# Two matmul layers behind a decayed attention: a planner that ranks by simulated passes and also places TensorE's steps

## The chip, the core and the metric

The kernel runs on one core of a Trainium2 chip. The metric is the device time of one launch, in microseconds; the median of three runs before the change is 581.78 us (581.52 to 581.89). "Profile" is one execution recorded by the hardware profiler. The engines are PE (TensorE), DVE (VectorE), ACT (ScalarE), POOL (GpSimd) and SP (SyncE, which here only starts transfers). Each takes its instructions strictly in the order in which the program put them.

## The reference, cut to what matters

Attention first, in blocks of 64 positions with a decayed running state, over 2 batches, 8 heads, 768 positions and a head size of 64:

```python
for b in range(nb):                       # 12 blocks of 64
    intra = (qb @ kb.T * Dmask) @ vb
    inter = (qb * lam_pow) @ kv_state
    out[block b] = intra + inter
    kv_state = lam_block * kv_state + (kb * rev_pow).T @ vb
x = out as 1536 tokens x 512
h = x @ w_in;  g = where(h > 0, h, exp(min(h, 0)) - 1);             x = g @ w_out    # layer 0
h = x @ w_in;  g = max(h, 0) + alpha * min(h, 0);                   x = g @ w_out    # layer 1
```

`w_in` is 512x2048 and `w_out` 2048x512 in both layers. Everything is float32; the kernel gets the products' precision from three passes over operands split into a high and a low part (hi*hi, hi*lo, lo*hi), names ending in `h` and `l`.

## The kernel before

**Attention** runs in six units `m` of 128 positions of both batches. Each unit has four steps on PE: `scores` (L557, 32 matmuls of 64x64), `state` (L604), `outputs` (L644) and `earlier` (L668, the part that comes from the running state, in two pieces of 16). Around them DVE multiplies scores by the mask (`sm`, L565) and adds to the state (L630), ACT or POOL decays the state (L623, L626), POOL scales keys and queries (`kd` L575, `qs` L586), ACT and DVE split the result into high and low parts (`qbh` L374, `qbl` L696, `x0h`, `x0l`). The trace shows two records for each 64x64 matmul, and a weight load record for each.

**The layers.** Tokens are in three tiles `t` of 512. Up products of tile 0 (and of all tiles for the first weight step `j`=0) are plain: groups of six 128x512 matmuls (L815, operands `x0` or `qb`, weights `wa`). Tiles 1 and 2 otherwise share seven products of a Strassen-like scheme (L845): A11, A12, S1, S2, S4, S3, A22 in that order, where the S products use `ws` (weight sums) and `qT1` to `qT3` (token differences). DVE joins their banks in L859; ACT and DVE apply the activation (L762, L773, L775, L779) and split it (`g`, high part by ACT L374, low part by POOL or DVE L382). Down products (L895) read `g` and `wd`, and DVE adds their banks to `acc` (L906). Weights arrive as 64-bit words (`raw`, L362) and are converted by ACT L408 and DVE L410, L413, L416 into `wt`, then split into `wa`, `wd`, `ws` (L374, L382). At the start of each layer `combine` subtracts quarters of `acc` (acc<-acc, L382) and splits the results into `qT1` to `qT3`.

**Order.** The program first only lists steps (`Plan.add`), each with a cost for every engine that could take it. `needs` walks back from the end and gives each step the latest time at which it may start; PE's own steps are a fixed chain in the order in which the program listed them, which `merge` laid out by hand (up products and down products in turn). `run` then plays the steps forward once: each engine but PE takes the ready step that is needed first, PE takes its next one in the list. DVE and POOL exclude one another on steps marked `shared`. Two rules steer POOL and DVE: POOL holds back from a step if DVE has a more urgent shared one due within `HOLD` (8 us), and DVE leaves a step to POOL while it has more than `SPARE` (8 us) of slack. What `run` emits is the program.

Of the kernel before, what the change touches and what calls it, by code (L numbers as in the profile page):

```python
# [43 lines left out]
class Op:  # L44
    def __init__(self, costs, run, late, shared, dma):
        self.costs, self.run, self.late, self.shared, self.dma = costs, run, late, shared, dma
        self.least = min(costs.values())
        self.after, self.before = set(), []
        self.heir, self.waits = None, 0
        self.left = 0  # L50
        self.need = 0.0
        self.begun = False


class Plan:

    LAT = 0.12
    SPARE = 8.0  # L60
    EASE = 0.3
    HOLD = 8.0
# [6 lines left out]
    def add(self, costs, run, reads=(), writes=(), late=0.0, shared=False, dma=False):  # L69
        op = Op(costs, run, late, shared, dma)  # L70
# [12 lines left out]
    def behind(self, a, b):  # L83

        a.heir, b.waits = b, 1

    def needs(self):

        pe = [op for op in self.ops if "PE" in op.costs]
        behind = dict(zip(pe, pe[1:]))  # L90
        left = {}
        for op in self.ops:
            for a in op.after:
                a.before.append(op)
        for op in self.ops:
            left[op] = len(op.before) + (op in behind) + (op.heir is not None)
        todo = [op for op in self.ops if not left[op]]
        ahead = dict(zip(pe[1:], pe))
        first = {op.heir: op for op in self.ops if op.heir}
        n = 0  # L100
        while todo:
            op = todo.pop()
            n += 1
            ends = [s.need - (0.0 if "PE" in op.costs and "PE" in s.costs else self.LAT)
                    for s in op.before]
            if op in behind:
                ends.append(behind[op].need)
            op.need = min(ends, default=0.0) - op.least - op.late
            if op.heir:
                op.need = min(op.need, op.heir.need - op.least)  # L110
            for a in [*op.after, *([ahead[op]] if op in ahead else []),
                      *([first[op]] if op.waits else [])]:
                left[a] -= 1
                if not left[a]:
                    todo.append(a)
        assert n == len(self.ops)
        return pe

    def run(self):
        pe = self.needs()  # L120
        for op in self.ops:
            op.left = len(op.after) + op.waits
# [3 lines left out]
        events, n = [], 0  # L126
        at, done, now, dma, shift = 0, 0, 0.0, 0.0, -pe[0].need
# [13 lines left out]
        def begin(e, op):  # L141
            nonlocal dma
            op.begun = True
            op.run(e)
            if op.heir:
                op.heir.left -= 1
                if not op.heir.left:
                    offer(op.heir)
            cost = op.costs[e]
            free[e] = now + cost  # L150
# [3 lines left out]
            if op.dma:  # L154
                dma = max(dma, now + 1.6) + op.late
                wake(dma + self.LAT, op)
            else:
                wake(now + cost + (0.0 if e == "PE" else self.LAT), op)

        for op in self.ops:  # L160
            if not op.left:
                offer(op)
        while done < len(self.ops):
            for e in self.ENGINES:
                if free[e] > now + 1e-9:
                    continue
                if e == "PE":
                    if at < len(pe) and not pe[at].left:
                        shift = now - pe[at].need
# [4 lines left out]
                while ready[e]:  # L174
                    item = heapq.heappop(ready[e])
                    op = item[2]
                    if op.begun:
# [4 lines left out]
                    if e == "POOL" and any(  # L182
                            x.shared and not x.begun and x is not op and x.need < op.need
                            and x.need + shift < now + op.costs[e] + self.HOLD for _, _, x in ready["DVE"]):
# [3 lines left out]
                    slack = op.need + shift - now  # L188
# [10 lines left out]
            while events and events[0][0] <= now + 1e-9:  # L199
# [4 lines left out]
                for s in op.before:  # L204
                    s.left -= 1
                    if not s.left:
                        offer(s)

# [18 lines left out]
def attention_two_layers(  # L227
# [124 lines left out]
    def pe(cost, run, reads, writes):  # L352
        return plan.add({"PE": cost}, lambda e: run(), reads, writes)
# [144 lines left out]
    ATT = 0.95  # L498
# [51 lines left out]
    def scores(m):  # L550

        ks = two_banks(m, 0)
        for b, x in enumerate(units[m]):
# [7 lines left out]
            pe(ATT / 2, run, [x.b_kq], [b_ps[k] for k in ks])  # L561
# [31 lines left out]
    def state(m):  # L593
# [14 lines left out]
        pe(ATT, run, [*b_kd[m % 2], *[x.b_v for x in units[m]]], [b_ps[k] for k in ks])  # L608
# [27 lines left out]
    def outputs(m):  # L636
# [13 lines left out]
        pe(ATT, run, [*b_sm[m % 2], *[x.b_v for x in units[m]]], [b_ps[k] for k in ks])  # L650
# [8 lines left out]
    def earlier(m, ks):  # L659

        for s in range(2):
            k = ks[s]
            if m or s:
# [10 lines left out]
                last[m] = pe(ATT / 2, run, [b_st[(2 * m + s) % 4], *b_qs[m % 2]], [b_ps[k]])  # L674
# [436 lines left out]
```

## Time and profile before

| | |
|---|---|
| median of three runs | 581.78 us |
| the profiled execution, as timed | 581.23 us |
| its span in the trace | 579.3 us |
| PE busy | 550.4 us, 95% of the span |
| DVE, ACT, POOL busy | 383.0, 293.1, 339.2 us |
| the chain of work that ended last | PE 85%, DVE 9% of the span |

The profiled execution was timed 1.9 us above its span and 0.55 us below the median. PE is the engine with the least idle time, so the page is to be read by asking where PE stands still, and behind whom. The 40 slices show it idle in the first four (attention), and full from the fifth to the last but for single tenths.

### The profile page before, as it was taken

How to read it: one execution, taken by the hardware profiler on the slowest of the kernel's cores; microseconds unless marked ns; L12 is line 12 of the kernel's file. 1: busy time of each engine (PE TensorE's matmuls, PEld its weight loads, DVE VectorE, ACT ScalarE, POOL GpSimd, SP SyncE). 2: the span in 40 equal slices, each digit the busy share in tenths (PEclk: the TensorE clock that was granted, in tenths of full speed). 3: DMA queues.
4: the chain of work that ended last, by engine and by line, in shares of the span. 5: the costliest groups of instructions: out<-in, count | busy, mean ns of one | idle time of the engine just before them, and what ended most of it. 6: DMA issues, size and time to landing. Idle time of an engine off the chain costs nothing.

```text
span 579.3 us, 9092 instructions
## 1 busy us (share of the span) xinstructions
PE 550.4 (95%) x3712; PEld 457.1 (79%) x3712; DVE 383.0 (66%) x494; ACT 293.1 (51%) x474; POOL 339.2 (59%) x231
## 2 busy tenths in 40 slices
PE   7557999899999999999999999999999999999997
PEld 6457787788888888888878878788888888888886
DVE  3346679955866675757884688467776776765464
ACT  2326668585746464646562554664453443534320
POOL 4457152658767566564475886767859293946020
PEclk9778999999999999999999999999999999999999
DMA  8992032103122212221240100222332222000013
GB/s 320 393 291 77 20 129 74 46 30 143 41 106 74 72 74 72 74 72 74 72 147 1 35 39 1 73 74 73 98 120 74 72 74 72 1 0 1 36 38 145
DMA packets 20012, 49.62 MB, mean 86 GB/s; under 512 B 1282, under 2 KB 1538, under 8 KB 19970
## 3 DMA queue, kind: packets, MB, share of 16 engines
q1 hardware_dynamic: 19696, 48.51, 24.3%
q8 instruction: 29, 0.48, 0.3%
q10 hardware_dynamic: 274, 0.52, 0.3%
q14 instruction: 13, 0.11, 0.1%
HBM read 45.88 MB, written 3.15 MB: 85 GB/s over the span
## 4 chain that ended last, share of the span: by engine, by line
PE 85%; DVE 9%; issue 4%; DMA 1%; ACT 1%; SPq 0%; ACTq 0%
PE ps L895 41%; PE ps L845 20%; PE ps L815 18%; PE ps L668 2%; PE ps L604 1%; PE ps L557 1%; PE ps L644 1%; DMA blk<-in_vk 1%; DVE g L382 1%; DVE wt L413 1%; DVE qbl L382 1%; DVE wt L416 1%; DVE wdl L382 1%; DVE ps L859 1%; DVE acc L906 1%
## 5 line engine op out<-in xcount | busy, mean ns | idle before, releaser
L906 DVE TENSOR_TENSOR acc<-ps,acc 128x512 f32<-128x512 f32 (+1 forms) x169 | 116.1, 687 | 93.5 <-PE ps L895 92.6
L382 POOL TENSOR_TENSOR g<-rt,g 128x512 fp32r<-128x512 f32 x81 | 121.2, 1503 | 90.1 <-ACT g L374 88.0
L895 PE MATMUL ps<-wdh,g 128*128 128x512 f32 (+1 forms) x388 | 118.7, 387 | 1.4 <-DVE g L382 1.4
L895 PE MATMUL ps<-g,wdh 128*128 128x512 f32 x384 | 118.3, 389 | 0.0
L762 ACT ACTIVATE rt<-ps 128x512 f32<-128x512 f32 x96 | 57.3, 599 | 107.8 <-DVE ps L859 62.6
L895 PEld LDWEIGHTS ps<-wdh,g 128*128 128x128 f32 x388 | 72.7, 188 | 16.7 <-DVE g L382 1.9
L895 PEld LDWEIGHTS ps<-g,wdh 128*128 128x128 f32 x384 | 72.1, 188 | 15.0
L895 PE MATMUL ps<-wdl,g 128*128 128x512 f32 (+1 forms) x194 | 75.1, 387 | 0.0
L895 PE MATMUL ps<-g,wdl 128*128 128x512 f32 x192 | 74.8, 390 | 0.2 <-DVE wdl L382 0.2
L374 ACT CAST g<-rt 128x512 fp32r<-128x512 f32 x96 | 59.3, 618 | 28.7 <-DVE rt L775 14.4
L382 POOL TENSOR_TENSOR wsl<-wt,wsh 128x1024 fp32r<-128x1024 f32 x13 | 32.3, 2484 | 48.1 <-ACT wsh L374 30.5
L779 DVE SCALAR_TENSOR_TENSOR rt<-rt,beta,ps 128x512 f32<-128x512 f32 x48 | 35.7, 744 | 30.2 <-ACT rt L762 30.1
L382 POOL TENSOR_TENSOR wt<-wt 128x256 f32<-128x256 f32 x54 | 41.1, 778 | 10.4 <-DVE wt L416 4.8
L416 DVE SCALAR_TENSOR_TENSOR wt<-raw,wt 128x1024 uint32<-128x1024 uint32 x32 | 46.3, 1450 | 0.0
L413 DVE SCALAR_TENSOR_TENSOR wt<-raw,wt 128x1024 uint32<-128x1024 uint32 x32 | 45.6, 1429 | 0.2
L374 ACT COPY ut<-ps 128x512 f32<-128x512 f32 x42 | 24.6, 587 | 36.3 <-PE ps L845 36.1
L382 POOL TENSOR_TENSOR wdl<-wt,wdh 128x1024 fp32r<-128x1024 f32 x13 | 37.2, 2861 | 8.9 <-ACT wdh L374 8.7
L895 PEld LDWEIGHTS ps<-g,wdl 128*128 128x128 f32 x192 | 36.0, 188 | 7.9 <-DVE wdl L382 0.6
L895 PEld LDWEIGHTS ps<-wdl,g 128*128 128x128 f32 x194 | 36.4, 188 | 7.4
L859 DVE TENSOR_TENSOR ps<-ps,ut 128x512 f32<-128x512 f32 x42 | 29.2, 697 | 14.5 <-PE ps L845 14.3
L815 PE MATMUL ps<-x0l,wah 128*128 128x512 f32 x128 | 38.8, 389 | 0.0
L775 DVE SCALAR_TENSOR_TENSOR rt<-rt,ps 128x512 f32<-128x512 f32 x48 | 32.5, 681 | 8.7 <-ACT rt L773 8.0
(116 smaller groups left out, 948.6 us busy)
## 6 DMA issues: line engine op xcount, KB each, us to landing
raw<-in_w1i SPq DMA_DIRECT2D x8, 1024.0 KB, 5.5
raw<-in_w1o SPq DMA_DIRECT2D x8, 1024.0 KB, 4.9
raw<-in_w2i SPq DMA_DIRECT2D x8, 1024.0 KB, 5.5
raw<-in_w2o SPq DMA_DIRECT2D x8, 1024.0 KB, 4.9
blk<-in_kqT SPq DMA_DIRECT2D x11, 512.0 KB, 10.8
blk<-in_vk SPq DMA_DIRECT2D x10, 512.0 KB, 10.9
out<-acc SPq DMA_DIRECT2D x11, 256.0 KB, 2.0
blk<-in_kqT ACTq DMA_DIRECT2D x1, 512.0 KB, 5.3
```

Source lines behind the costliest of these rows:

```text
L374: nc.scalar.copy(dst(), src())
L382: lambda e: on(e).tensor_tensor(out=dst(), in0=a(), in1=b(), op=alu),
L413: op({"DVE": vec(1024)}, lambda e: nc.vector.scalar_tensor_tensor(out=tu, in0=lower, scalar=29, in1=tu, op0=ALU.logical_shift_right, op1=A ...
L416: op({"DVE": vec(1024)}, lambda e: nc.vector.scalar_tensor_tensor(out=tu, in0=upper, scalar=0x80000000, in1=tu, op0=ALU.bitwise_and, op1=A ...
L762: op({"ACT": act(512, True)}, lambda e: nc.scalar.activation(rt(i), h(), AF.Relu, scale=-1.0), [b_h], [b_r])
L775: op({"DVE": vec(512)}, lambda e: nc.vector.scalar_tensor_tensor(out=rt(i), in0=rt(i), scalar=-1.0, in1=h(), op0=ALU.add, op1=ALU.max), [b ...
L779: op({"DVE": vec(512) + 0.06}, lambda e: nc.vector.scalar_tensor_tensor(out=rt(i), in0=rt(i), scalar=beta[:, f:f + 1], in1=h(), op0=ALU.mu ...
L815: nc.tensor.matmul(out=banks[k], lhsT=wa(s, w)[:, cc, q * 128:(q + 1) * 128], rhs=(both[t][x] if t else x0(x))[:, cc, :], start=i == 0, st ...
L845: nc.tensor.matmul(out=banks[k], lhsT=left(s, a, w)[:, cc, :], rhs=quad(b, x)[:, cc, :], start=bool(opens and i == 0), stop=bool(closes an ...
L859: op({"DVE": vec(512)}, lambda e: nc.vector.tensor_tensor(out=banks[to], in0=banks[k], in1=ut(u), op=ALU.add), [b_ps[k], b_ut[u]], [b_ps[to]])
L895: nc.tensor.matmul(out=p_, lhsT=lhs, rhs=rhs, start=i == 0, stop=i == 5)
L906: op({"DVE": vec(w)}, lambda _, a=a, p_=p_: nc.vector.tensor_tensor(out=a(), in0=p_, in1=a(), op=ALU.add), [b_ps[k], *b_a], b_a)
```

## The change

The planner is rewritten; the kernel's mathematics, tiles and costs of the other engines stay.

- `needs` is used for a first ranking only. Then six rounds follow: a forward simulation, then one backwards through the same rules, whose start times become the ranks of the next round. The forward pass that ended first in the model is emitted.
- With `FREE`, PE takes the ready step with the lowest rank instead of the next in the list.
- Instruction fetch enters the model: a PE step has a number of instructions (`steps`: 12 for six 128x512 matmuls, 128 for 32 of 64x64), the model holds 512 ahead and refills 80 per us, and a step whose instructions are missing costs more.
- `SPARE` goes from 8 to 5 us and `HOLD` from 8 to 2 us, and the cost of 32 small matmuls, `ATT`, from 0.95 to 0.88 us.

```diff
-    SPARE = 8.0
+    SPARE = 5.0
     EASE = 0.3
-    HOLD = 8.0
+    HOLD = 2.0
+    ROUNDS = 6
+    FETCH = 80.0
+    AHEAD = 512.0
+    FREE = True
...
             for e in op.costs:
-                if e != "PE":
-                    heapq.heappush(ready[e], (op.need, n, op))
+                if e != "PE" or self.FREE:
+                    heapq.heappush(ready[e], (first[op], n, op))
...
             cost = op.costs[e]
+            if op.steps:
+                stock = min(self.AHEAD, stock + self.FETCH * (now - seen))
+                cost = max(cost, (op.steps - stock) / self.FETCH)
+                stock, seen = stock + self.FETCH * cost - op.steps, now + cost
...
+                if e == "PE" and self.FREE:
+                    while ready[e]:
+                        op = heapq.heappop(ready[e])[2]
+                        if op not in begun:
+                            shift = now - first[op]
+                            begin(e, op)
+                            break
+                    continue
...
+    def run(self):
+        self.pe = [op for op in self.ops if "PE" in op.costs]
+        for op in self.ops:
+            for a in op.after:
+                a.before.append(op)
+        first, best = self.needs(), None
+        for _ in range(self.ROUNDS):
+            log = []
+            begun, end = self.simulate(first, log=log)
+            if best is None or end < best[0]:
+                best = end, log
+            begun, end = self.simulate({op: -t for op, t in begun.items()}, True)
+            first = {op: -t - op.least - op.late for op, t in begun.items()}
+        for e, op in best[1]:
+            op.run(e)
...
-    def pe(cost, run, reads, writes):
-        return plan.add({"PE": cost}, lambda e: run(), reads, writes)
+    def pe(cost, run, reads, writes, steps=12):
+        return plan.add({"PE": cost}, lambda e: run(), reads, writes, steps=steps)
...
-    ATT = 0.95
+    ATT = 0.88
```

What that moves is seen in the emitted order; line numbers of the new program are 40 higher. Three places follow.

**PE, from the last units of attention to the first layer products**, before (from unit 3's `outputs`, over `earlier` of unit 3 and unit 4's steps):

```order
L644 MATMUL ps<-sm,blk 64x64 x32
L557 MATMUL ps<-blk 64x64 x32
L668 MATMUL ps<-qs,dmst 64x64 x16
L668 MATMUL ps<-qs,stqp 64x64 x16
L604 MATMUL ps<-blk,kd 64x64 x32
L644 MATMUL ps<-sm,blk 64x64 x32
L557 MATMUL ps<-blk 64x64 x32
L815 MATMUL ps<-qbh,wah 128x512 x4
L815 MATMUL ps<-qbl,wah 128x512 x2
L668 MATMUL ps<-qs,dmst 64x64 x16
```

and in the new program, from unit 4's `outputs`:

```order
L684 MATMUL ps<-sm,blk 64x64 x32
L708 MATMUL ps<-qs,stqp 64x64 x16
L597 MATMUL ps<-blk 64x64 x32
L644 MATMUL ps<-blk,kd 64x64 x32
L708 MATMUL ps<-qs,dmst 64x64 x32
L855 MATMUL ps<-qbh,wah 128x512 x4
L855 MATMUL ps<-qbl,wah 128x512 x4
L855 MATMUL ps<-qbh,wal 128x512 x4
```

Both `earlier` pieces of unit 4 (L668, now L708) moved ahead of the first layer product, 24 layer matmuls (the three rows and the same three once more) now stand in a row where six stood, and the layer products are broken by attention steps three times instead of six. `outputs` (L644, now L684) mostly comes before `state` (L604, now L644).

**DVE, at the step from layer 0's `j`=0 to `j`=1** (`wsl` is the low part of the weight sums that the S products read, `acc<-acc` the subtractions of `combine`), before:

```order
L382 TENSOR_TENSOR g_1254<-rt,g_1254 128x512
L382 TENSOR_TENSOR wdl<-wt,wdh 128x1024
L382 TENSOR_TENSOR wsl<-wt,wsh 128x1024
L382 TENSOR_TENSOR acc<-acc 128x2x256 x3
L906 TENSOR_TENSOR acc_1231<-ps,acc_1231 128x512
L859 TENSOR_TENSOR ps<-ps,ut 128x512
```

and in the new program:

```order
L422 TENSOR_TENSOR qT1l<-acc,qT1h 128x2x256 x2
L450 TENSOR_SCALAR wt<-wt 128x1024
L422 TENSOR_TENSOR wsl<-wt,wsh 128x1024
L453 SCALAR_TENSOR_TENSOR wt<-raw,wt 128x1024
L815 SCALAR_TENSOR_TENSOR rt<-rt,ps 128x512
L456 SCALAR_TENSOR_TENSOR wt<-raw,wt 128x1024
L422 TENSOR_TENSOR g_1262<-rt,g_1262 128x512
L416 CAST wdh<-wt 128x1024
L422 TENSOR_TENSOR acc<-acc 128x2x256
L422 TENSOR_TENSOR wdl<-wt,wdh 128x1024
L422 TENSOR_TENSOR acc<-acc 128x2x256 x3
```

`wsl` moved ahead of the third weight conversion, and seven of the eight subtractions of this `combine` are now DVE's (three before; POOL had five). On PE, S1 follows the last `x0` product after five groups of six matmuls (A11 and four downs) where it followed after eight.

**PE and DVE at the change of layers.** PE at the end of layer 0, from its last S3 (qT3), before:

```order
L845 MATMUL ps<-qT3h,wsh 128x512 x2
L845 MATMUL ps<-qT3l,wsh 128x512 x2
L845 MATMUL ps<-qT3h,wsl 128x512 x2
L895 MATMUL ps<-g_1061,wdh 128x512 x2
L895 MATMUL ps<-g_1061,wdl 128x512
L895 MATMUL ps<-g_1179,wdh 128x512 x2
L895 MATMUL ps<-g_1179,wdl 128x512
L845 MATMUL ps<-qbh,wah 128x512 x2
```

and in the new program:

```order
L885 MATMUL ps<-qT3h,wsh 128x512 x2
L885 MATMUL ps<-qT3l,wsh 128x512 x2
L885 MATMUL ps<-qT3h,wsl 128x512 x2
L935 MATMUL ps<-g_1044,wdh 128x512 x2
L935 MATMUL ps<-g_1044,wdl 128x512
L935 MATMUL ps<-g_1166,wdh 128x512 x2
L935 MATMUL ps<-g_1166,wdl 128x512
L935 MATMUL ps<-g_1207,wdh 128x512 x2
L935 MATMUL ps<-g_1207,wdl 128x512
L935 MATMUL ps<-g_1262,wdh 128x512 x2
L935 MATMUL ps<-g_1262,wdl 128x512
L885 MATMUL ps<-qbh,wah 128x512 x2
```

DVE some 35 us later, where layer 1 begins, before:

```order
L906 TENSOR_TENSOR acc<-ps,acc 128x512
L382 TENSOR_TENSOR wdl<-wt,wdh 128x1024
L382 TENSOR_TENSOR qbl<-acc,qbh 128x512
L382 TENSOR_TENSOR g_1254<-rt,g_1254 128x512
L906 TENSOR_TENSOR acc_1231<-ps,acc_1231 128x512
```

and in the new program:

```order
L946 TENSOR_TENSOR acc<-ps,acc 128x512
L422 TENSOR_TENSOR qbl<-acc,qbh 128x512
L422 TENSOR_TENSOR g_1211<-rt,g_1211 128x512
L422 TENSOR_TENSOR qbl<-acc,qbh 128x512
L422 TENSOR_TENSOR acc<-acc 128x1024
L422 TENSOR_TENSOR qbl<-acc,qbh 128x512
L422 TENSOR_TENSOR acc<-acc 128x1024
L946 TENSOR_TENSOR acc_1242<-ps,acc_1242 128x512
```

A22 (`qbh,wah`) now has two groups of downs between itself and S3 instead of one. The `wdl` that stood at the head of DVE's queue is POOL's now; six shared steps stand there in place of three.

DVE has 500 instructions where it had 494, POOL 226 where it had 231. The transfers on SP keep their order but for one pair of weight loads, and the output transfers and last 17 down products stand as before.

## Rows read from the trace of the kernel before

**Rows 1.** The page's first part: busy time of each engine.

```profile
PE 550.4 (95%) x3712; PEld 457.1 (79%) x3712; DVE 383.0 (66%) x494; ACT 293.1 (51%) x474; POOL 339.2 (59%) x231
```

**Rows 2.** Windows: stretch, length, busy time and records by engine, clock, DMA.

```profile
12.92:58.76 45.84, 27.65 (x1067) 26.19 (x1061) 20.41 (x30) 20.27 (x55) 26.87 (x22) 0.78 0.72 253
58.76:78.15 19.39, 19.14 (x277) 14.65 (x273) 14.10 (x18) 11.57 (x23) 7.67 (x4) 1.00 0.18 57
78.15:116.00 37.85, 36.13 (x158) 29.32 (x157) 33.90 (x43) 25.82 (x43) 16.55 (x12) 1.00 0.24 75
116.00:293.00 177.00, 177.00 (x782) 146.60 (x781) 120.67 (x155) 106.47 (x161) 108.18 (x73) 1.00 0.22 74
368.50:576.20 207.70, 207.68 (x922) 172.03 (x921) 134.44 (x171) 86.81 (x129) 119.08 (x79) 1.00 0.18 63
```

**Rows 3.** PE's waits: waiting line, releaser, total us, times, longest.

```profile
PE ps L557 <- issue: 12.5, 5, 5.7
PE ps L604 <- issue: 4.1, 2, 3.2
```

**Rows 4.** PE's timeline in attention: start, us, records; in brackets the wait.

```profile
21.72 0.80 PE L604 MATMUL ps<-blk,kd 64*64 64x64 f32 x18 [3.21 <-issue]
22.21 2.01 PE L644 MATMUL ps<-sm,blk 64*64 64x64 f32 x64
23.91 1.50 PE L557 MATMUL ps<-blk 64*64 64x64 f32 x46
28.19 0.80 PE L557 MATMUL ps<-blk 64*64 64x64 f32 x18 [2.77 <-issue]
...
42.31 0.80 PE L557 MATMUL ps<-blk 64*64 64x64 f32 x18 [5.75 <-issue]
...
50.62 0.51 PE L557 MATMUL ps<-blk 64*64 64x64 f32 x19 [1.00 <-issue]
...
58.25 0.57 PE L557 MATMUL ps<-blk 64*64 64x64 f32 x23 [1.28 <-issue]
```

**Rows 5.** The page's DMA queues: packets, MB, share of 16 engines.

```profile
q8 instruction: 29, 0.48, 0.3%
```

**Rows 6.** Windows of 10 us, columns as in rows 2.

```profile
20.00:30.00 10.00, 5.51 (x172) 5.32 (x173) 3.03 (x5) 2.31 (x8) 6.68 (x7) 0.52 1.03 394
40.00:50.00 10.00, 7.32 (x254) 7.18 (x255) 5.11 (x8) 3.72 (x11) 4.34 (x3) 0.66 0.21 60
...
100.00:110.00 10.00, 10.00 (x46) 8.29 (x45) 10.00 (x11) 5.06 (x9) 7.44 (x5) 1.00 0.00 0
```

**Rows 7.** The chain that ended last, 60 to 120 us: start, us, records.

```profile
60.94 1.08 PE ps L668 x32
62.02 1.58 PE ps L815 x6
...
112.97 1.62 PE ps L845 x6
...
117.33 1.36 PE ps L895 x6
```

**Rows 8.** Timelines of PE and DVE, 60 to 120 us.

```profile
89.03 0.61 PE L895 MATMUL ps<-g,wdh 128*128 128x512 f32 x2
...
100.37 0.62 PE L845 MATMUL ps<-qT1h,wsh 128*128 128x512 f32 x2
...
97.60 1.89 DVE L382 TENSOR_TENSOR acc<-acc 128x512 f32<-128x512 f32 x3
```

**Rows 9.** Timelines of DVE and PE at the change of layers.

```profile
296.13 1.97 DVE L416 SCALAR_TENSOR_TENSOR wt<-raw,wt 128x1024 uint32<-128x1024 uint32 x1
...
298.77 0.73 PE L845 MATMUL ps<-qbh,wah 128*128 128x512 f32 x2 [0.56 <-DVE ps L859]
...
333.99 2.59 DVE L382 TENSOR_TENSOR wdl<-wt,wdh 128x1024 fp32r<-128x1024 f32 x1 [0.17 <-ACT wdh L374]
...
342.24 0.50 PE L895 MATMUL ps<-wdh,g 128*128 128x512 f32 x1 [1.45 <-DVE g L382]
```

More of the change, by code (lines that the diff above doesn't have):

```diff
@@ L44, with __init__, __hash__ @@
 class Op:
-    def __init__(self, costs, run, late, shared, dma):
+    def __init__(self, n, costs, run, late, shared, dma, steps):
+        self.n = n
         self.costs, self.run, self.late, self.shared, self.dma = costs, run, late, shared, dma
+        self.steps = steps
         self.least = min(costs.values())
         self.after, self.before = set(), []
[L49 to L52, printed above, removed]
+        self.heir = self.lead = None
+    def __hash__(self):
+        return self.n
 class Plan:
     LAT = 0.12
-    SPARE = 8.0
+    SPARE = 5.0
     EASE = 0.3
-    HOLD = 8.0
+    HOLD = 2.0
[3 more added lines that the diff above has]
+    FREE = True
     ENGINES = ("PE", "SP", "ACT", "DVE", "POOL")
@@ L115, in needs, with simulate @@
                     todo.append(a)
[L116 to L120, printed above, removed]
+        assert len(need) == len(self.ops)
+        return need
+    def simulate(self, first, back=False, log=None):
+        pe = self.pe[::-1] if back else self.pe
+        before = (lambda op: op.after) if back else (lambda op: op.before)
+        left = {op: len(op.before if back else op.after) for op in self.ops}
         for op in self.ops:
-            op.left = len(op.after) + op.waits
+            if (op.heir if back else op.lead):
+                left[op] += 1
         ready = {e: [] for e in self.ENGINES}
@@ L153, in begin @@
             wake(free[e])
-            if op.dma:
+            if back:
+                next_, gap = op.lead, cost
+            else:
+                next_, gap = op.heir, 0.0
+            if next_:
+                left[next_] -= 1
+                if not left[next_]:
+                    offer(next_)
+            if op.dma and not back:
                 dma = max(dma, now + 1.6) + op.late
@@ L157, in begin @@
             else:
-                wake(now + cost + (0.0 if e == "PE" else self.LAT), op)
+                wake(now + cost + op.late * back + (0.0 if e == "PE" else self.LAT), op)
         for op in self.ops:
-            if not op.left:
+            if not left[op]:
                 offer(op)
@@ L166, in run @@
                     continue
+                if e == "PE" and self.FREE:
[6 more added lines that the diff above has]
+                    continue
                 if e == "PE":
[L168 to L169 removed]
+                    if at < len(pe) and not left[pe[at]]:
+                        shift = now - first[pe[at]]
                         begin(e, pe[at])
@@ L182, in run @@
                     if e == "POOL" and any(
-                            x.shared and not x.begun and x is not op and x.need < op.need
-                            and x.need + shift < now + op.costs[e] + self.HOLD for _, _, x in ready["DVE"]):
+                            x.shared and x not in begun and x is not op and first[x] < first[op]
+                            and first[x] + shift < now + op.costs[e] + self.HOLD
+                            for _, _, x in ready["DVE"]):
                         held.append(item)
@@ L203, in run @@
                 done += 1
-                for s in op.before:
-                    s.left -= 1
-                    if not s.left:
+                for s in before(op):
+                    left[s] -= 1
+                    if not left[s]:
                         offer(s)
+        return begun, now
+    def run(self):
[13 more added lines that the diff above has]
+            op.run(e)
 def act(n, psum=False):
```

61 lines of the change are left out of this document (26 added, 35 removed).

## The prediction, made before the changed kernel ran

> **What bounds the kernel now.** I read the busy times first: PE works 550.4 of 579.3 us [rows 1], so only its 28.9 idle us and what makes its work longer can be won. The windows by stage say where they lie [rows 2]. In the attention, 12.92 to 58.76 us, PE is busy 27.65 of 45.84 us: 18.2 idle. From 58.76 to 78.15 it lacks 0.25, from 78.15 to 116 it lacks 1.7. In the rounds of the layers it lacks nothing: 177.00 of 177.00 us, later 207.68 of 207.70. So no order of the rounds can gain there; it can only lose.
>
> Of the attention's idle time 12.5 and 4.1 us, 16.6 in all, are put down to "issue" [rows 3], a wait for nothing that the trace names. The timeline shows what it is [rows 4]. After the wait that ends at 21.72 PE runs 18, 64 and 46 matmul records, 128, and waits again. Each has a weight load beside it, so 256 instructions lie between waits, and PE's 7424 instructions over the 29 packets of the instruction queue are 256 a packet [rows 1, 5]. These are waits for code. They come at fixed instruction counts, whatever the instructions are. From 42.31 to 50.62 and on to 58.25 PE ran two packets each time, 8.3 and 7.6 us, while the waits shrank from 5.75 to 1.00 and 1.28 us [rows 4]. From 20 to 30 us the input loads fill the DMA (share 1.03), from 40 to 50 they don't (0.21); TensorE's granted clock, which is full elsewhere, is 0.52 in the first of these, so mostly at its 1.2 GHz level, after the long waits [rows 6].
>
> On this the Trainium skill speaks against the planner's new term: the page "Runtime: NRT & Kernel Launch", section "Instruction fetch mechanics", says that instructions come in 16 KiB blocks of 256 and that crossing a block is mostly hidden. The block size agrees with the trace; the hiding doesn't, at 16.6 us of waits. By the page the waits would not be fetch and a new order could shed them, which is the last rival below.
>
> **The change part by part.** The planner itself costs nothing on the chip; it emits nearly the same instructions in another order. So four places are costed, and the tail: from 576.20 to 579.3 nothing differs, 0.
>
> *Attention.* The new order must fetch the same code. Both `earlier` pieces of unit 4, 64 records, are now ahead of the first layer product. There they cost half a packet at the late pace, 7.6/4 = 1.9 us [rows 4], and they no longer cost 2 times 1.08 = 2.16 us behind it [rows 7]: -0.26. Each return from small matmuls to layer products makes a group of six take 1.58 us instead of 1.36 [rows 7]; three returns instead of six give -0.66. `earlier`'s second piece now stands behind `state` of its own unit and waits for DVE's addition to it, a step of 0.63 us [rows 8], of which its first piece (half of 1.08) covers most: +0.3 with the way between the engines. The 0.25 us that PE lacked from 58.76 on goes, since DVE's `qbl` is now covered by two pieces of `earlier`. Some `outputs` now directly follow their own scores and want the masks, two DVE steps of 0.63; they stand where code is late anyway, and I put them at 0. Sum -0.9. Bounds: half of the last three waits of rows 4 gone on top, -4.0 more; a wait for masks (1.3 us) in two packets and not covered, +2.6 more.
>
> *Step to `j`=1.* PE now lacks 1.7 us here and runs one group in 1.62 instead of 1.36 after the wait for L859, together 2.0 [rows 2, 7]. In the new order S1 comes five groups after the last `x0` product, 6.8 us, where it came 100.37 - 89.03 = 11.3 us after it [rows 8]. `wsl` must be there by then; it ended before 97.60, that is 8.6 us after 89.03. From the first `x0l` to `wsl` DVE's queue holds 34 instructions before and 33 now: two weight conversions and two `wdl` less, one `wal` and two `qT1l` more. At 0.63 us for a 512-wide step [rows 8] and, estimated, twice that for a 1024-wide one that is 2.5 us less, so `wsl` should come at 6.1 us, just ahead of S1. What follows it is later instead: four subtractions more on DVE at 1.89/3 = 0.63 are 2.5 us, with DVE already busy 10.00 of 10 us [rows 6]. I take 1.6 us of waits for the 2.0: -0.4. Bounds -2.0 (no wait) and +2.6 (the third rival).
>
> *Change of layers.* A22 waited 0.56 us at 298.77 because DVE's L859 stood behind a weight conversion of 1.97 us [rows 9]; with its dearer restart that is 0.8. One more group, 1.36 us, now lies between S3 and A22 and covers it: -0.8. At 342.24 PE waited 1.45 us for a `g` low part [rows 9], the last of three shared DVE steps of which `wdl` took 2.59 us beside POOL. `wdl` went to POOL, ahead of the steps of `combine` there, and `g` moved up by one place: -1.45 and 0.2 of restart. What is late next is the row of six shared steps; the addition behind them frees a bank that PE wants 11 groups, 15.0 us, after the addition ahead of them. At 0.63 us for the narrow ones and twice that for the wide they are through in 5.0 us; at 2.59 each, as beside POOL [rows 9], in 15.5, with the two additions 16.9, which is 1.9 too late. POOL cannot stand beside all of them, so I put 0.55 us of new waits there. Sum -1.9. Bounds -2.5 (none) and +0.9 (1.9 here and one more like that of 342.24).
>
> *The rounds.* PE lacks nothing in either layer's rounds [rows 2], and in the new order each product still follows its operands by as many groups as before. 0, with +1.5 as the upper bound, one wait like that of 342.24.
>
> Sum: -0.9 - 0.4 - 1.9 = -3.2. The profiled execution was timed at 581.23, so 578.0 for it; the median of the runs stands 0.55 higher, so **578.6 us**.
>
> **The rivals.**
>
> *The code waits shrink too.* If the new order leaves less small work between two packets late in the attention, the next packet is asked for sooner. For it: a wait grew or shrank with what PE ran before it, 2.77 and 5.75 against 1.00 and 1.28 [rows 4]. Against it: the number of packets before the first layer product grows by half a one. Half of the 8.0 us in the last three waits of rows 4 is -4.0: 574.6 us.
>
> *Nothing is left of it.* The late gain comes back as waits in the new queue of six shared steps and at S1, and the attention, bound by packets, ends as before. For it: every place gained is a wait of DVE's queue that hangs on tenths of a microsecond. 581.5 us.
>
> *Slower: S1 overtakes DVE.* The place is 95 us. If `wsl` ends as long after the last `x0` product as before (8.6 us), and the four subtractions push the L859 and `wdl` steps behind them back by 2.5 us, PE waits 8.6 - 6.8 + 2.5 + 0.3 = 4.6 us instead of 2.0, +2.6. It decides from where `wsl` ends later than 6.8 us after that product. With DVE that late, the planner's other tight places are no better: the change of layers gains nothing. 581.78 - 0.9 + 2.6 = 583.5 us. Against it: DVE's queue ahead of `wsl` is shorter.
>
> *The waits aren't code.* Then order can shed those that end after 40 us, when the loads no longer fill the DMA [rows 6]: 8.0 us of them [rows 4], 581.8 - 8.0 - 3.2 = 570.6 us. The count of 128 records speaks against it. This is what the rule of the Trainium skill's page above would give.
>
> **How the numbers follow.** Forecast 0.50 (576.6 to 580.6 by itself), shrinking code waits 0.15, nothing 0.15, S1 late 0.17, waits not code 0.03. A measurement of this kernel can tell about 0.2%, 1.2 us, from no change. Faster by more than that, under 580.6: most of the first, 0.47, with 0.15 and 0.03, and of "nothing" 0.02: 0.67. Slower, over 582.9: of S1 late 0.14 and of "nothing" 0.02: 0.16. The rest, 0.17, is within. The range of 574.2 to 583.4 leaves out 0.03 and 0.06 of the shrinking waits below, and 0.09 of the slower case above: 0.18.
>
> **What would show it.** In the trace after: the waits on "issue" still total 15 to 18 us and still come 128 or 256 records apart; the first layer product starts between 59 and 62 us and the first on `x0` about 1 us earlier than at 78.15; no wait of A22 on L859 before the change of layers and none of 1 us on a `g` after it; PE idle in the step to `j`=1 between 0.5 and 2.5 us. The prediction is wrong if "issue" falls below 10 us (then the order does move the fetch), if PE lacks more than 1 us within the rounds, or if S1 (qT1, wsh) waits for `wsl`.

## The result, and the profile after

The changed kernel runs at 574.59 us median (573.89 to 574.65, four runs) against 581.83 us before (581.52 to 581.89): 0.9874 of it, 95% interval 0.9857 to 0.9891, or 7.2 us less. Faster was forecast, at 578.6 with -3.2 us; the gain is over twice that, and the time lies at the low end of the range. The profiled execution is the lowest of its four, 573.89. Five kernels have PE's order up to the first `x0` product in common, this one and e1, e2, e5 and e13 below. They start that product at 75.3 to 76.2 us, so one profile tells the attention's end to about 1 us only.

The page's first part after, as in [rows 1]: PE is busy 1.0 us less, its idle time fell from 28.9 to 22.6 us.

```profile
span 572.0 us, 9090 instructions
...
PE 549.4 (96%) x3712; PEld 458.7 (80%) x3712; DVE 381.2 (67%) x500; ACT 293.5 (51%) x473; POOL 325.3 (57%) x226
```

Windows by stage after, cut where PE has done, to within one record of 0.23 us, as many records as at the cuts of [rows 2] (start and end; length, PE's busy time and records, the other engines', clock, DMA share, GB/s):

```profile
12.92:59.78 46.86, 31.04 (x1112) 29.15 (x1104) 22.49 (x33) 20.43 (x58) 20.84 (x19) 0.78 0.70 248
59.78:75.27 15.49, 15.49 (x213) 12.85 (x209) 10.94 (x14) 10.41 (x19) 2.32 (x2) 1.00 0.09 19
75.27:110.75 35.48, 35.48 (x158) 29.37 (x157) 33.83 (x46) 25.24 (x43) 14.32 (x8) 1.00 0.22 82
110.75:287.75 177.00, 177.00 (x783) 146.56 (x782) 124.65 (x158) 109.09 (x164) 113.78 (x77) 1.00 0.24 78
287.75:361.20 73.45, 73.00 (x321) 59.82 (x320) 51.06 (x60) 39.42 (x61) 54.36 (x33) 1.00 0.17 58
361.20:568.90 207.70, 207.69 (x922) 172.01 (x921) 131.37 (x170) 86.66 (x128) 113.81 (x78) 1.00 0.17 59
```

Of the kernel before, [rows 2] lacks the window at the change of layers:

```profile
293.00:368.50 75.50, 73.26 (x320) 59.65 (x320) 53.46 (x58) 39.26 (x62) 55.37 (x33) 1.00 0.13 43
```

Against [rows 2] and this line, length by length, this is the whole account:

| stage | before | after | difference | forecast |
|---|---|---|---|---|
| attention to the first layer product | ends 58.76 | ends 59.78 | +1.02 | +2.2 |
| first layer product to first `x0` product | 19.39 | 15.49 | -3.90 | -3.1 |
| step to `j`=1 | 37.85 | 35.48 | -2.37 | -0.4 |
| rounds of layer 0 | 177.00 | 177.00 | 0 | 0 |
| change of layers (before: 293.0 to 368.5) | 75.50 | 73.45 | -2.05 | -1.9 |
| rounds of layer 1 | 207.70 | 207.70 | 0 | 0 |
| sum, as the spans (579.3 to 572.0) | | | -7.30 | -3.2 |

These ends put 0.1 us of one stage into another. Followed matmul by matmul, the new kernel is 2.88 us ahead at the first `x0` product and 5.15 ahead behind the step (110.66 against 115.81). It is still 5.15 ahead at the end of layer 0's rounds, and 7.29 behind the change of layers. So the step gained 2.27, and the change of layers 2.14.

PE's waits after, as in [rows 3] (waiting line, releaser; total, times, longest). Behind the attention one is left, 0.39 us for L819 at 351.93; before there were five:

```profile
PE ps L644 <- issue: 5.4, 3, 3.2
PE ps L597 <- issue: 4.6, 2, 2.3
PE ps L684 <- issue: 3.3, 2, 2.4
...
PE ps L708 <- issue: 1.2, 1, 1.2
...
PE ps L885 <- DVE rt L819: 0.4, 1, 0.4
```

PE's timeline after, the steps that start a packet of code late in the attention, as in [rows 4], and the wait at 351.93 (start, us, records; the wait in brackets). The waits on "issue" total 5.4 + 4.6 + 3.3 + 1.2 = 14.5 us where they were 16.6:

```profile
42.66 1.08 PE L644 MATMUL ps<-blk,kd 64*64 64x64 f32 x50 [3.18 <-issue]
...
49.44 0.50 PE L644 MATMUL ps<-blk,kd 64*64 64x64 f32 x18 [0.68 <-issue]
...
53.34 0.74 PE L708 MATMUL ps<-qs,stqp 64*64 64x64 f32 x19 [1.23 <-issue]
...
57.34 0.51 PE L644 MATMUL ps<-blk,kd 64*64 64x64 f32 x19 [1.57 <-issue]
...
351.93 0.73 PE L885 MATMUL ps<-qT1h,wsh 128*128 128x512 f32 x2 [0.39 <-DVE rt L819]
```

### The profile page after: what moved, and what is told of

Its sections match the earlier page's. It is cut to its first block, busy times and chain, and to the rows that moved or that the text cites. A ratio compares the mean times of both kernels' runs of the same rounds, so it can differ in the third digit from the quotient of the medians.

```text
span 572.0 us, 9090 instructions
## 1 busy us (share of the span) xinstructions
PE 549.4 (96%) x3712; PEld 458.7 (80%) x3712; DVE 381.2 (67%) x500; ACT 293.5 (51%) x473; POOL 325.3 (57%) x226
## 4 chain that ended last, share of the span: by engine, by line
PE 92%; issue 3%; DVE 3%; DMA 1%; ACT 1%; SPq 0%; DVEq 0%; ACTq 0%
PE ps L935 45%; PE ps L885 22%; PE ps L855 18%; PE ps L708 2%; PE ps L684 2%; PE ps L597 2%; PE ps L644 2%; DMA blk<-in_kqT 1%; DVE qT2l L422 1%; DVE g L422 0%; DVE wt L456 0%; DVE acc L946 0%; DVE rt L819 0%; DVE sm L605 0%; ACT rt L802 0%
## 5 line engine op out<-in xcount | busy, mean ns | idle before, releaser
L422 POOL TENSOR_TENSOR g<-rt,g 128x512 fp32r<-128x512 f32 x86 | 123.4, 1440 | 74.6 <-ACT g L414 67.3
L422 POOL TENSOR_TENSOR wdl<-wt,wdh 128x1024 fp32r<-128x1024 f32 x14 | 40.3, 2878 | 28.3 <-ACT wdh L414 28.0
L819 DVE SCALAR_TENSOR_TENSOR rt<-rt,beta,ps 128x512 f32<-128x512 f32 x48 | 35.6, 743 | 25.3 <-ACT rt L802 25.3
L422 POOL TENSOR_TENSOR wt<-wt 128x256 f32<-128x256 f32 x50 | 37.8, 765 | 14.3 <-DVE wt L456 7.1
L456 DVE SCALAR_TENSOR_TENSOR wt<-raw,wt 128x1024 uint32<-128x1024 uint32 x32 | 45.2, 1416 | 0.0
L453 DVE SCALAR_TENSOR_TENSOR wt<-raw,wt 128x1024 uint32<-128x1024 uint32 x32 | 44.8, 1401 | 0.2
L899 DVE TENSOR_TENSOR ps<-ps,ut 128x512 f32<-128x512 f32 x42 | 29.2, 697 | 19.0 <-PE ps L885 17.6
L448 ACT ACTIVATE wt<-raw 128x1024 f32<-128x1024 f32 x32 | 36.5, 1140 | 5.7 <-POOL wt L422 3.2
```

The source lines that it names most:

```text
L422: lambda e: on(e).tensor_tensor(out=dst(), in0=a(), in1=b(), op=alu),
L448: op({"ACT": 1.14}, lambda e: nc.scalar.mul(t, upper.bitcast(F32), 2.0 ** -112), [b_r], [b_t])
L453: op({"DVE": vec(1024)}, lambda e: nc.vector.scalar_tensor_tensor(out=tu, in0=lower, scalar=29, in1=tu, op0=ALU.logical_shift_right, op1=A ...
L456: op({"DVE": vec(1024)}, lambda e: nc.vector.scalar_tensor_tensor(out=tu, in0=upper, scalar=0x80000000, in1=tu, op0=ALU.bitwise_and, op1=A ...
L819: op({"DVE": vec(512) + 0.06}, lambda e: nc.vector.scalar_tensor_tensor(out=rt(i), in0=rt(i), scalar=beta[:, f:f + 1], in1=h(), op0=ALU.mu ...
L899: op({"DVE": vec(512)}, lambda e: nc.vector.tensor_tensor(out=banks[to], in0=banks[k], in1=ut(u), op=ALU.add), [b_ps[k], b_ut[u]], [b_ps[to]])
```

## The experiments

All times are medians. The kernel before ran at 581.5 to 581.6 in these sessions, and each ratio is against it.

| run | us | ratio, 95% interval |
|---|---|---|
| e1 new attention, old rest | 581.62 | 0.9994 (0.9982 to 1.0005) |
| e2 new up to `j`=2, old rest | 576.51 | 0.9913 (0.9900 to 0.9926) |
| e3 old up to `j`=2, new rest | 579.13 | 0.9961 (0.9946 to 0.9977) |
| e4 before, A22 a group later, twice | 579.03 | 0.9960 (0.9946 to 0.9974) |
| e5 = e1 with e4's edit | 578.04 | 0.9938 (0.9923 to 0.9952) |
| e6 after, one packet of code more | 577.85 | 0.9928 (0.9909 to 0.9947) |
| e7 after, 4 MB of input loads less | 570.15 | 0.9799 (0.9781 to 0.9816) |
| e8 after, PE in the listed order | 581.84 | 1.0004 (0.9988 to 1.0021) |
| e9 = e4, `wdl` on POOL | 577.37 | 0.9922 (0.9909 to 0.9936) |
| e10 after, old SPARE and HOLD | 574.31 | 0.9870 (0.9850 to 0.9889) |
| e11 after, one round | 584.29 | 1.0045 (1.0029 to 1.0060) |
| e12 after, dearer fetch and `earlier` | 575.88 | 0.9895 (0.9879 to 0.9912) |
| e13 = e5, two `wdl` on POOL | 577.59 | 0.9928 (0.9916 to 0.9940) |
| e14 old, new step to `j`=1, old | 579.90 | 0.9971 (0.9960 to 0.9982) |

### The places apart, and together: e1, e2, e14, e3

One program makes both orders and emits the one up to a step and the other behind it. `run_old` is the planner of before on the same list of steps:

```diff
-        for e, op in best[1]:
+        new, old = best[1], self.run_old()
+        for e, op in self.joined(new, old):
             op.run(e)
+    def joined(self, new, old):
...
+        return follow(cut(new, (0, 0, 0, 0, 0)), old)
```

That is e1; the others cut at `(0, 2, 0, 0, 0)`, the first plain product of `j`=2, or at both.

> The new planner's order on all engines up to the first x0 product, the old planner's order from there on. The kernel before runs at 581.8 and the new one at 574.6; in the trace the new one reaches the first x0 product 78.15 - 75.27 = 2.9 us sooner. Theory, the gains lie in separate places and each is kept: 581.8 - 2.9 = 578.9. Rival, the attention's gain is handed back at S1 or A22 of j=1, because DVE's old queue there was only just in time for the later start: 580.5 or more, with waits of PE between 85 and 115 us that total over 3 us.

> The new planner's order up to the first plain product of j=2 of layer 0 (116 us), the old order from there on. Theory, separate places: the new kernel is 115.81 - 110.66 = 5.15 us ahead after the same number of layer products, so 581.8 - 5.15 = 576.7, and the two waits of the old order at the change of layers (0.56 and 1.45 us) are still there. Rival, the early gain comes back as waits in the old rounds: 578.5 or more.

> The old order up to the first x0 product, the new planner's order from there to the first plain product of j=2, the old order behind that. Theory, the new order of the step to j=1 loses nothing by itself: the waits of 0.16 and 1.56 us and their restarts go, 2.0 to 2.3 us, so 579.5, and the waits at the change of layers stay. Rival, it is fitted to the new attention: started from the old one DVE's queue comes out late against PE's new order and waits of over 1 us appear: 580.5 or more.

> The old planner's order up to the first plain product of j=2 of layer 0, the new order from there on. Theory, separate places: what is left of the 7.3 us, 7.3 - 5.15 = 2.15, so 579.7; the waits before 116 us as in the kernel before, none at the change of layers but about 0.4 us near 350. Rival, the new order of the change of layers depends on what the new early part leaves (which weights lie in which buffer): waits of over 1 us there and 581 or more.

e2, e14 and e3 came out as the theory of separate places had them, within 0.6 us. e1 didn't: its rival held. (e1's twelve times spread from 579.86 to 582.73.) With the step to `j`=1 the four make a square: old attention and old step 581.6, new attention alone 581.6, new step alone 579.9, both 576.5. The attention's gain is worth nothing in front of the old step and 3.4 us in front of the new one.

Where e1 lost it shows in PE's timeline at A22, of before and of e1 (L915; L929 is the line that was L859), and in the windows around it in e1 (columns as above). The profiled execution of e1, 582.49, is the second slowest of its twelve, so not every one need have lost as much:

```profile
112.97 0.70 PE L845 MATMUL ps<-qbh,wah 128*128 128x512 f32 x2 [1.56 <-DVE ps L859]
...
112.39 0.70 PE L915 MATMUL ps<-qbh,wah 128*128 128x512 f32 x2 [2.10 <-DVE ps L929]
112.92 0.66 PE L915 MATMUL ps<-qbl,wah 128*128 128x512 f32 x2
113.39 1.05 PE L915 MATMUL ps<-qbh,wal 128*128 128x512 f32 x2
114.23 1.06 PE L965 MATMUL ps<-g,wdh 128*128 128x512 f32 x2
```

```profile
112.39:113.40 1.01, 1.01 (x5) 0.84 (x6) 1.01 (x2) 1.01 (x3) 1.01 (x3) 0.99 0.53 97
113.40:116.70 3.30, 3.30 (x9) 2.65 (x8) 2.10 (x3) 1.82 (x4) 2.14 (x2) 0.50 0.83 286
```

The first `x0` product of e1 started at 75.96 instead of 78.15, 2.2 us sooner, but DVE released A22 only 0.6 us sooner, at 112.39 against 112.97: PE waited 2.10 instead of 1.56, after 0.94 for a `wdl` at 95.50. Then TensorE's clock stood at 0.50, its 1.2 GHz level, for 3.3 us. A22 and the group behind it took from 112.39 to 116.79, 4.40 us, where before they took 115.81 - 112.97 = 2.84; so 1.6 us more went. Behind A22 e1 is 1.0 us later than before.

Why DVE wasn't 2.2 us sooner too shows where it works beside POOL. The new attention leaves POOL's `wal` and a `qT1l` to 76.05 and 79.09, where the old one has them at 73.19 and 75.53. Two `g` steps of DVE now fall beside them. DVE's timeline, before and e1:

```profile
78.91 1.33 DVE L382 TENSOR_TENSOR g<-rt,g 128x512 fp32r<-128x512 f32 x2
...
77.39 4.01 DVE L450 TENSOR_TENSOR g<-rt,g 128x512 fp32r<-128x512 f32 x2
```

In e2, where DVE does that `wal` itself behind them, they take 1.29.

### A22's place, and DVE's load: e4, e5, e13

e4 takes the old order and lets A22 and the group of downs behind it change places, at `j`=1 and at the end of layer 0:

```diff
-            op.run(e)
+            log.append((e, op))
...
+        for j in (1, NU - 1):
+            a = next(i for i, x in enumerate(log) if getattr(x[1], "tag", None) == ("A22", 0, j))
+            b = next(i for i, x in enumerate(log) if i > a and x[0] == "PE")
...
+            log = log[:a] + kept + moved + log[b + 1:]
+        for e, op in log:
+            op.run(e)
```

> The kernel before with one edit at two places: in layer 0 at j=1 and at the last j, A22 stands behind the group of six downs that followed it; all other engines' orders unchanged. Theory, the waits of A22 vanish because one more group of 1.36 us lies between S3 and A22: at j=1 A22 would ask at 112.6 for what is there at 112.9, so the 1.56 us wait shrinks to 0.2 to 0.4, and the 0.56 us at the end of layer 0 goes; with restarts 1.3 + 0.8, so 579.7. Rival, what counts is DVE's queue and not PE's distance: the wait moves to the next product that needs DVE and the time stays at 581.3 to 582.

Held, with 2.5 us for 2.1 expected. In e4's timeline A22 asks 1.4 us later for what came at 112.97 before:

```profile
112.99 0.70 PE L855 MATMUL ps<-qbh,wah 128*128 128x512 f32 x2 [0.22 <-DVE ps L871]
```

The new planner has the same at `j`=1. PE's timeline after: two groups of downs (each row pair is half a group) between S3 and A22, and no wait; DVE's timeline shows the steps of L899 done at 109.92:

```profile
107.94 0.62 PE L935 MATMUL ps<-g,wdh 128*128 128x512 f32 x2
...
109.97 0.62 PE L935 MATMUL ps<-g,wdh 128*128 128x512 f32 x2
110.43 0.39 PE L935 MATMUL ps<-g,wdl 128*128 128x512 f32 x1
110.66 0.62 PE L885 MATMUL ps<-qbh,wah 128*128 128x512 f32 x2
```

```profile
108.64 1.28 DVE L899 TENSOR_TENSOR ps<-ps,ut 128x512 f32<-128x512 f32 x2
```

> The new attention in front of the old order (which by itself ran at 581.6 against 581.6 of the kernel before), and besides A22 moved behind one more group of downs at j=1 and at the end of layer 0 (which by itself ran at 579.0). Theory, DVE's queue sets A22 at j=1: DVE reached the L859 step that A22 waits for only 0.6 us sooner with the new attention (111.55 against 112.13), so 579.0 - 0.6 = 578.4; the wait of A22 falls from 2.10 to about 0.75 us and TensorE's clock, 0.50 for 3.3 us after the 2.10 us wait, stays at 1.0. Rival, with A22 moved the whole 2.2 us that x0 starts sooner are kept: 576.8.

Held: 578.0 for 578.4. A22 waits 0.72 us at 111.84, the clock isn't lost, but of the attention's gain only 579.0 - 578.0 = 1.0 us arrives. So A22's place isn't all; DVE comes too late there, its two `g` steps again taking 3.99 us.

e13 takes work from DVE: of `e5` the first `wdl` of layer 0 and the second of layer 1 are emitted on POOL.

```diff
-            op.run(e)
+            op.run("POOL" if getattr(op, "tag", None) == "wdl" else e)
```

> The run of new attention with A22 moved (578.0), and besides two steps taken from DVE to POOL: layer 0's first wdl (DVE did it for 1.21 us at 80.75) and layer 1's second wdl (worth 1.65 by itself). Theory, at j=1 the order counts and not the amount of DVE's work: DVE stands idle for 0.66 us at 88.26 for a weight conversion of ACT, so 1.2 us less work ahead of that ends up as more idle time, the waits of 0.94 and 0.72 us at 95 and 112 us stay, and only the change of layers gains: 578.0 - 1.65 = 576.4. Rival, DVE's load is what hands the attention's gain back: both waits go, with their restarts 2.0 us more, 574.4, as much as the whole change.

577.6 is neither: 1.2 above the theory, far from the rival's 574.4. At `j`=1 the run doesn't decide between them, for DVE's load was not lowered. On POOL `wdl` took 2.88 us, from 79.93 on, and POOL's next steps then ran beside DVE's, which grew (a `g` of 1.61 and one of 1.77 us). From the first `x0` product to the conversion L486, DVE was busy 11.94 us, in e5 12.12. Its idle time there is as in e5, not 1.2 us more, as the theory had it (DVE's timelines, e5 and e13):

```profile
88.26 0.69 DVE L486 TENSOR_SCALAR wt<-wt 128x1024 uint32<-128x1024 uint32 x1 [0.66 <-ACT wt L484]
...
89.97 0.69 DVE L486 TENSOR_SCALAR wt<-wt 128x1024 uint32<-128x1024 uint32 x1 [0.65 <-ACT wt L484]
```

PE waits 0.27 us for a `g` at 88.44, 0.38 for `wdh` and 0.94 for `wdl` at 95 to 97 us (in e5 the 0.94 alone), and the first `x0` product came later in this execution (76.22 against 75.40). The wait for A22 is 0.22 us, and the 1.45 us wait at the change of layers is gone, as expected. So whether less work for DVE would keep the attention's gain is not shown. The new planner keeps it (e2 against e14), and what differs there is the order: on PE, S1 and A12 stand ahead of the downs that need the next `wdl`; on DVE, `wsl` stands ahead of the conversion that leads to it, and the two `g` steps aren't beside POOL's `wal`. Which of these carries it was not tried apart, and stays open.

### The change of layers: e9

> The kernel before with A22 moved at its two places (by itself 579.0) and with the low part of layer 1's second down weights, wdl, done by POOL where DVE did it; every other place in every queue unchanged. In the trace with A22 moved alone, DVE worked 2.60 us on wdl from 331.77, ahead of qbl and of the g that PE waits 1.45 us for at 340. Theory, wdl ahead of g is that wait: it goes, with 0.2 us of restart, and 579.0 - 1.65 = 577.4. Rival, POOL now does acc, wsl and qT1l 2.5 us later and the wait comes back there or on g itself, which stays stretched beside POOL: 578.5 to 580.

The edit is e13's, on e4 and for layer 1's step alone. 577.37 for 577.4 expected. DVE's timeline of e9 shows `qbl` and `g` still stretched beside POOL (2.47 and 2.88 us), but `g` ends at 337.54 and PE asks for it at about 338.6:

```profile
332.26 2.47 DVE L392 TENSOR_TENSOR qbl<-acc,qbh 128x512 fp32r<-128x512 f32 x1 [0.69 <-ACT qbh L384]
334.66 2.88 DVE L392 TENSOR_TENSOR g<-rt,g 128x512 fp32r<-128x512 f32 x1
```

### Whether the waits are code: e6, e7

e6 repeats unit 5's scores, e7 lets units 3 and 4 read blocks that are there already:

```diff
-                for pr in range(NP):
+                for pr in [*range(NP)] * (3 if m == 5 else 1):
```

```diff
-             homes(in3, b_in[3]), homes(blk[0:4], b_g[0:4]), homes(in5, b_in[5])]
+             homes(in2, b_in[2]), homes(blk[0:4], b_g[0:4]), homes(in5, b_in[5])]
...
-        fetch(3)
...
-                fetch(4)
```

> The new kernel, with the 32 matmuls of unit 5's scores done three times over into the same banks (64 matmuls, 128 records, 256 instructions more, near 55 us); the order is unchanged. Theory, the late attention is bound by packets of code: two packets took 57.34 - 49.44 = 7.90 us, so one more costs 3.95 and the time is 574.6 + 3.95 = 578.5. Rival, the waits on issue are not code: PE pays only its own time for 128 such records, 2 x 0.91 = 1.8 us, less what the 1.23 and 1.57 us waits there take up, so 574.6 to 576.4.

+3.3 us, near the theory (+3.95) and outside the rival's 0 to 1.8. PE's timeline of e6 settles it:

```profile
53.20 0.74 PE L708 MATMUL ps<-qs,stqp 64*64 64x64 f32 x19 [1.23 <-issue]
...
56.65 1.44 PE L597 MATMUL ps<-blk 64*64 64x64 f32 x83 [1.02 <-issue]
...
60.10 0.51 PE L644 MATMUL ps<-blk,kd 64*64 64x64 f32 x19 [1.36 <-issue]
```

The wait that stood ahead of the last 19 records of L644 now stands in the middle of the repeated scores, 128 records behind the one before, and ahead of those 19 records of L644 there is a new one, 128 records further. A packet took 3.45 us here.

> The new kernel without the input loads of units 3 and 4, 4 MB of 12: these units read again the blocks of units 2 and 0. The order of PE is the same. Theory, code arrives late up to 41 us because the input loads fill the DMA: they now end some 10 us sooner, from about 31 us on the packets come at the late pace of 3.95 us, and the first layer product, which now stands at 59.8 us, comes at about 55: 569 to 571 in all. Rival, a packet takes as long with idle DMA, what bounds the attention is a chain of its own steps: first layer product within 1 us of 59.8 and 574 to 575.

570.15, as the theory had it, and the first layer product at 53.13 instead of 59.78. But PE's order did not stay the same: the planner, run anew, put one `earlier` piece of unit 4 (32 records) behind the first layer product, and attention steps break the layer products four times, not twice. So 53.13 flatters. The first `x0` product, with the whole attention ahead of it in both orders, comes at 70.34, 4.9 us sooner. With the loads gone PE's waits on "issue" total 10.3 us instead of 14.5, and none of them lies between 30 and 43 us, where there were 0.90 and 3.18. So the input loads do delay code.

### The planner's parts: e8, e10, e11, e12

```diff
-    FREE = True
+    FREE = False
```

> The new planner with PE kept to the listed order (ranks, SPARE, HOLD and the six rounds as in the new one). Theory, the gain is PE's new order: the attention's gain (2.9 us) is gone, A22 at j=1 again stands one group behind S3 and waits, so 580 to 583. Rival, the ranks alone make DVE and POOL serve the old PE order without waits: 577 or less.

```diff
-    SPARE = 5.0
+    SPARE = 8.0
...
-    HOLD = 2.0
+    HOLD = 8.0
```

> The new planner with SPARE and HOLD back at 8 and 8 us. Theory, PE's freedom is the gain and these two constants only shift a few shared steps between DVE and POOL: the first x0 product within 1 us of 75.3, up to 1.5 us of waits more behind it, so 574.6 to 577. Rival, the constants carry the step to j=1 (DVE takes the subtractions, POOL no longer holds back): A22 waits there for over 1 us again and the time is 577.5 or more.

```diff
-    ROUNDS = 6
+    ROUNDS = 1
```

> The new planner with one forward pass alone, its ranks those of the backward walk along the listed PE order, PE free. Theory, ranks from passes in which the engines compete are needed: with the old ranks DVE's queue at the step to j=1 is as late as before and A22 or S1 waits, 578 to 584. Rival, PE's freedom alone is enough: 574 to 576.

Without PE's freedom nothing is left of the gain (581.84), without the later rounds the kernel is slower than before (584.29, just above the range expected), and the two constants change nothing in the total that can be measured (574.31). `ATT` was not tried apart. PE's timeline of e11 shows the slow rival of the forecast at its place, S1 waiting for `wsl`, and the window behind it the clock (a second wait, 2.76 us for a `g`, ends at 344.28):

```profile
100.32 1.22 PE L885 MATMUL ps<-qT1h,wsl 128*128 128x512 f32 x2 [2.71 <-DVE wsl L422]
```

```profile
100.32:101.30 0.98, 0.98 (x2) 0.83 (x3) 0.98 (x1) 0.95 (x1) 0.00 (x0) 0.50 0.92 376
```

```diff
-    FETCH = 80.0
-    AHEAD = 512.0
+    FETCH = 55.0
+    AHEAD = 256.0
...
-                last[m] = pe(ATT / 2, run, [b_st[(2 * m + s) % 4], *b_qs[m % 2]], [b_ps[k]], 64)
+                last[m] = pe(1.0, run, [b_st[(2 * m + s) % 4], *b_qs[m % 2]], [b_ps[k]], 64)
```

> The new planner with costs as the traces show them: fetch 55 instructions per us with 256 ahead (a packet of 256 took 3.5 to 4 us), and a piece of earlier 1.0 us instead of 0.44 (32 records take 1.08 in the trace). With the values as they are, 80 and 512, the emitted order is row for row the one that comes out when fetch isn't counted at all. Theory, the planner now puts layer products between the last small matmuls where code is awaited, the first x0 product comes 1 to 2.5 us before 75.3, and 572.2 to 573.8 results. Rival, DVE's queue at the step to j=1 cannot follow the earlier start and hands it back as waits of A22 or S1, as in the run with the new attention alone: 574.5 or more.

The rival's time came out, 575.9, with a wait of 1.25 us at 100.02. It is S4's, though (`qbh,wsh`), for a copy by ACT that had waited for DVE's L899. Besides, the first `x0` product came 1.6 us later, not sooner. e12's order has again six returns from small matmuls to layer products and both `earlier` pieces of unit 4 behind the first one. The chain shows the two orders side by side, e12 first (start, us, records), then after:

```profile
58.05 1.59 PE ps L855 x6
59.63 1.08 PE ps L708 x32
60.71 1.58 PE ps L855 x6
62.30 1.08 PE ps L708 x32
```

```profile
65.51 1.01 PE ps L644 x29
...
66.59 0.93 PE ps L684 x62
67.52 1.59 PE ps L855 x6
69.11 2.01 PE ps L708 x64
71.13 7.02 PE ps L855 x30
```

The fetch term as the change has it, 80 and 512, moves nothing: with the term made ineffective the program emitted is the same, row for row on every engine. It is part of the change and no part of the gain.

## Why the prediction was wrong, step by step

Two terms of the sum failed by about 2 us each, the attention and the step to `j`=1. Part of the first is chance; the second is a step of the reasoning.

*Attention, -0.9; measured -2.9.* The order has to fetch the same code: right, the waits are code (e6). The half packet at 1.9 us: right; from the last packet's arrival to the first layer product it is 59.78 - 57.34 = 2.44 us where it was 58.76 - 58.25 = 0.51, +1.93. The +0.3 for a wait on DVE's addition did not come; PE has no such wait there.

Two terms were mis-sized. Behind the first layer product I put two pieces, three returns and one wait, 2.16 + 0.66 + 0.25 = 3.07. But the order breaks the layer products twice, not three times as I had read it, so there are four returns fewer; and pieces moved together cost less (two of 32 records take 2.01 us, not 2.16). Six breaks of 1.08 became two of 2.01: 6.49 - 4.02 = 2.47, with 4 x 0.22 = 0.88 for returns, and the remaining 0.55 of the 3.90 for the wait and its restart.

And ahead of it I took every pair of packets as alike. Here the pair from 42.31 on (42.66 after) took 8.31 us before and 6.78 after, -1.5, which nothing in my sum had. PE was busy for most of both; the granted clock there was 0.67 and 0.75 (I had called it full outside 20 to 30 us), with one `earlier` piece less in it. I don't count that as the order's doing: in e1, with the same order that far, the pair took 8.23 us, and in e14, with the old one, 7.42. It is part of why the attention's gain is 2.9 us in this execution and 1.9 to 2.75 in the other four of that order.

*Step to `j`=1, -0.4; measured -2.37, by the matmuls 2.27.* This is the step that failed. I asked whether `wsl` would come in time for S1 and carried 1.6 us of waits over because DVE was full, without a product that would wait. None did: PE was busy 35.48 of 35.48 us. `wsl` ended at 90.98, 2 us ahead of S1 at 92.95, a margin that I had put at 0.7 (DVE's and PE's timelines after):

```profile
89.77 1.21 DVE L422 TENSOR_TENSOR wsl<-wt,wsh 128x1024 fp32r<-128x1024 f32 x1
...
92.95 0.62 PE L885 MATMUL ps<-qT1h,wsh 128*128 128x512 f32 x2
```

And the wait of before was A22's for L859, as I had read it, but the new order puts two groups of downs between S3 and A22 at this place too. I counted that at the change of layers and not here. e4 measures it alone: the wait falls from 1.56 to 0.22.

*That the steps add up.* I added the attention's gain as if it were kept. It is kept only with the step's new order: 0.0 in e1, 1.0 in e5, 3.4 between e14 and e2. Had the step gone as I forecast, with waits left on DVE, e1 and e5 suggest that most of the attention's gain would have been lost there, and -3.2 would have been too much.

*Change of layers, -1.9; measured -2.05, by the matmuls -2.14.* Right, and by its reasons: A22's place (e4: no wait there) and `wdl` ahead of `g` (e9: 579.03 to 577.37, 1.66 for the 1.65 put on it). The new wait of 0.55 is 0.39 us at 351.93 (shown above). It too is for a bank, but one that L819 (`rt<-rt,beta,ps`) has to read first, not the addition.

*Rounds and tail, 0.* Right: the lead stays at 5.15 us through layer 0's rounds and at 7.3 through layer 1's.

*The rivals and signs.* Shrinking code waits named the time, 574.6, by luck, and not the cause: the late waits went from 8.0 to 3.18 + 0.68 + 1.23 + 1.57 = 6.7 us while one more came, and what was gained lay elsewhere. S1 late is what e11 does. That the waits aren't code fell with e6. The Trainium skill's page "Runtime: NRT & Kernel Launch", section "Instruction fetch mechanics", has the 256 instructions right, but crossings are not mostly hidden here: 14.5 us of waits after, and 3.3 us for one block more in e6. Of the signs, the place of the first layer product and the waits that should go held. Missed were "issue" (14.5 us for 15 to 18), the first `x0` product (2.9 us earlier for about 1) and PE's idle time in the step (none for 0.5 to 2.5).

## What to carry to other kernels

A gain ahead of a place where another engine is just in time can be worth nothing until that place moves too, as in e1: follow an earlier start to the next wait, and price the two together. Where a product waits for a step on another engine, count the groups between its producer and itself at every place where the pattern occurs, in the new order as in the old. A planner's term is worth a look at whether it changes the order at all: here the fetch term changed nothing, and a dearer one made the kernel slower.

## What the runs showed of the hardware that was not expected

A wait can cost more than its length once it is long: TensorE's clock fell from full to 0.50 after waits of 2.10 us (e1), 2.71 and 2.76 us (e11) and 2.35 us in e8, whose windows are below, each in a stretch of layer products. Each was seen in one execution. It stayed at 1.00 after 1.56 and 1.45 us before the change and after 1.25 in e12. In e1 that was 1.6 us on top of the wait.

```profile
339.50:341.94 2.44, 0.09 (x1) 0.00 (x0) 2.44 (x2) 0.00 (x0) 1.84 (x1) 0.98 0.01 3
341.94:343.00 1.06, 1.06 (x3) 0.87 (x4) 1.06 (x2) 0.00 (x0) 0.00 (x0) 0.50 0.00 0
```

And 4 MB less of input loads brought the first `x0` product 4.9 us forward (e7), though PE waited for an input only once after the change, 1.1 us at the start. PE's waits for code fell by 4.2 us: what the loads held up was mostly the code. How much of the 4.9 us is the order, which changed too, was not tried apart.
